# A recurrent attention loop on one core: the last K copied and transposed in two halves, one mask copy moved forward

## The chip, the cores and the metric

The kernel runs on one core of one Trainium2 chip. The metric is the device time of one execution in microseconds; runs of the same kernel are compared by their median. In the profile, PE is TensorE's matmuls, PEld its weight loads, DVE is VectorE, ACT is ScalarE, POOL is GpSimd and SP the engine that issues most DMAs. All times are microseconds unless marked ns; L495 is line 495 of the kernel.

## The reference, cut to what matters

Two blocks on `x` of 2048 tokens by 512. The first, which holds the change, is attention over segments of 32 tokens with a memory of 8 tokens that each segment hands to the next. With the shapes put in (32 heads of 128, 64 segments):

```python
mask = (idx[:, None] < M) | (idx[:, None] >= idx[None, :])   # L = 8 + 32 = 40 positions
mem = mem0
for s in range(n_seg):                                       # 64 segments, one after the other
    h = concatenate([mem, x[:, s*32:(s+1)*32]], axis=1)
    q, k, v = (einsum('btd,dhe->bhte', h, W) for W in (Wq, Wk, Wv))
    p = softmax(where(mask, einsum('bhqe,bhke->bhqk', q, k) * scale, -1e9))
    o = einsum('bhte,hed->btd', einsum('bhqk,bhke->bhqe', p, v), Wo)
    mem = o[:, :8]
    outs.append(o[:, 8:])
h = x + concatenate(outs)           # x goes into the loop layer-normed
```

The second block is a gated MLP with a 2048 by 2048 mixing over tokens: `h + ((z1 * (w_sp @ layernorm(z2) + b_sp)) @ w_out)` with `z1, z2` the halves of `gelu(layernorm(h) @ w_in)`. Everything is bf16 in memory.

## The kernel before, in words

The kernel is one straight list of operations. A small recorder (`Emitter`) takes each with the engine that it runs on and the tokens that it reads and writes, and puts a semaphore wait where a token's last writer or reader was on another engine. Within an engine the order is the order of the code, so what stands ahead of an operation on its queue is set by hand. A token of a PSUM bank, `("ps", bank)`, also makes a reader on one engine wait for earlier readers on another.

After a start phase the loop over the 64 segments begins (L926). Each of them depends on the one before by the 8 memory rows (`hT`, columns 0 to 7). Heads are worked on in two halves b = 0 and 1 of 16 heads each. One segment does, in this order of code:

1. **Q and K** (`QK`, L501): for each half, Q and K of the 8 memory rows and the segment's first 24 tokens (the last 8 tokens' projections are made for 16 segments at a time by the filling work), 16 matmuls of 512 columns each. Four matmuls go to four column groups of TensorE at a time. The bank is `QKB[(b, mi)]`: 0 for Q of half 0, 1 for K of half 0, 6 and 7 for half 1.
2. **Copy and transposition** (`QK_evac`, L512): ScalarE copies the bank from PSUM into `Tst` in bf16, in an order of columns that puts two heads into one 32-bit word (L515). VectorE then transposes the words, 32 by 32 at a time, into `QT` (L521) or `KT` (L524). `Tst` has one buffer for Q and one for K. This happens four times in a segment: Q0, K0, Q1, K1; K1 is the "last K".
3. **Mask** (`mask_put`, L534): VectorE writes the mask into the bank in which the scores of that half are then summed: bank 0 for half 0 and bank 1 for half 1, free again once Q0 and K0 have been copied. Half 0's mask copy stands after the transposition of Q0. Half 1's stands after that of Q1.
4. **Scores of half 0** (`S_half`, L538; matmuls L546 and L552), **exp of half 0** (L560, ScalarE), V matmuls (`V_half`), the softmax **sums of half 0** (L567 and the held ones at L496, TensorE, with a matrix of ones), **ln of half 0** (L578).
5. **Scores of half 1**, **exp of half 1**, then the reciprocal of half 0's sums as an exp (L582), the rest of V's half 1, **sums of half 1**, ln and reciprocal of half 1.
6. Normalising of the probabilities: half 0 on POOL, half 1 on VectorE (L586, L590). Ahead of half 0's POOL also copies the next segment's part of `QT` (L531), after the scores have read the old one.
7. A filling piece of other work for TensorE (projections for later segments, or parts of the second block), then **P·V** of both halves (L615, L621), their copies (`cT`), the output projection `Wo`, and the memory rows for the next segment.

In the first segment whole groups of V matmuls stand between the last K and the scores of half 0. After the loop comes the second block's mixing, which the change does not touch.

ScalarE's queue around the change is: copies of Q0, K0, Q1, K1, exp 0, ln 0, exp 1, reciprocal 0, ln 1, reciprocal 1. VectorE's queue is: transposition of Q0, mask 0, transposition of K0, transposition of Q1, mask 1, transposition of K1, copy of V 0, copy of V 1, normalising of half 1.

Of the kernel before, what the change touches and what calls it, by code (L numbers as in the profile page):

```python
# [8 lines left out]
U32 = mybir.dt.uint32  # L9
ACT = mybir.ActivationFunctionType  # L10
# [159 lines left out]
def fast_path(nc, st, keep, A_x, A_mem0, A_Wq, A_Wk, A_Wv, A_Wo, A_seg_len, B_w_in, B_w_sp, B_b_sp, B_w_out, out):  # L170
# [26 lines left out]
    def sb(name, shape, dt):  # L197
        return st.enter_context(nc.sbuf_tensor("f_" + name, shape, dt))
# [18 lines left out]
    QT = sb("QT", [128, 2, 8, 40, 2], BF)  # L217
    KT = sb("KT", [128, 2, 8, 32, 2], BF)
    Tst = sb("Tst", [128, 2, 512], BF)
# [40 lines left out]
    ps = st.enter_context(nc.psum_tensor("f_ps", [128, 8, 512], F32))  # L260
# [5 lines left out]
    def PB(b):  # L266
        return ("ps", b)
# [4 lines left out]
    def pe(fn, **k):  # L272
        return em.add("pe", fn, **k)

    def act(fn, **k):
        return em.add("act", fn, **k)

    def dve(fn, **k):
        return em.add("dve", fn, **k)
# [221 lines left out]
    def QK(s, b, mi, dcs, first, last, held=None):  # L501
        ws = (w_q, w_k)[mi]
        bank = QKB[(b, mi)]
        sl = slot(s)
        for dc in dcs:
            for c in range(4):
                rhs = ws[:, dc, :].rearrange("p (h c i) -> p c h i", c=4, i=32)[:, c, 16 * b:16 * b + 16, :]
                pe(lambda e, dc=dc, c=c, rhs=rhs: tile_mm(e, ps[32 * c:32 * c + 32, bank, :], hT[:, sl, dc, :], rhs,
                                                          dc == first, dc == last, c, dc == held),
                   reads=[("hTx", (s // 4) % 3), ("hTm", s, dc // 2), ("W", mi, 2 * b), ("W", mi, 2 * b + 1)], writes=[PB(bank)])  # L510

    def QK_evac(s, b, mi):  # L512
        bank = QKB[(b, mi)]
        tb = mi
        act(lambda e: e.activation(out=Tst[:, tb, :].rearrange("p (hp i r) -> p hp i r", i=32, r=2),  # L515
                                   in_=ps[:, bank, :].rearrange("p (hp r i) -> p hp i r", r=2, i=32), func=ACT.Copy),
            reads=[PB(bank)], writes=[("T", tb)])
        src = Tst[:, tb, :].bitcast(U32)
        if mi == 0:
            dst = QT[:, b, :, :, :].rearrange("p hp q r -> p (hp q r)").bitcast(U32).rearrange("p (hp q) -> p hp q", hp=8)[:, :, 8:40]  # L520
            dve(lambda e: e.transpose(out=dst, in_=src), reads=[("T", tb)], writes=[("QT", b)])  # L521
        else:
            dst = KT[:, b, :, :, :].rearrange("p hp q r -> p (hp q r)").bitcast(U32)
            dve(lambda e: e.transpose(out=dst, in_=src), reads=[("T", tb)], writes=[("KT", b)])  # L524

    def qx_copy(s):
        j = s % CK
# [6 lines left out]
    def mask_put(b):  # L534
        bank = SBK[b]
        dve(lambda e: e.tensor_copy(out=ps[:, bank, 0:224], in_=mask[:, :]), reads=["mask"], writes=[PB(bank)])  # L536

    def S_half(s, b):  # L538
        bank = SBK[b]
        j = s % CK  # L540
        buf = (s // CK) % 2
        rd = [("QT", b), ("KT", b), ("QTe", b)]
        for g in range(4):
            for c in range(4):
                hp, r = 2 * c + g // 2, g % 2
                pe(lambda e, hp=hp, r=r, c=c, g=g: e.matmul(  # L546
                    ps[32 * c:32 * c + 32, bank, g * 40:(g + 1) * 40], lhsT=KT[:, b, hp, :, r], rhs=QT[:, b, hp, :, r],
                    start=False, stop=(g == 3), skip_group_check=True, tile_position=(0, 32 * c)),
                    reads=rd, writes=[PB(bank)])
        for c in range(4):  # L550
            h0 = 16 * b + 4 * c
            pe(lambda e, c=c, h0=h0: e.matmul(  # L552
                ps[32 * c:32 * c + 32, bank, 160:224], lhsT=QTx[buf][:, 1, j, h0:h0 + 4, :].rearrange("p h k -> p (h k)"),
                rhs=QT[:, b, 2 * c:2 * c + 2, 0:16, :].rearrange("p hp q r -> p hp r q"),
                start=False, stop=True, skip_group_check=True, tile_position=(0, 32 * c)),
                reads=rd + [("QTx", buf, 1, i) for i in range(8)], writes=[PB(bank)])
# [369 lines left out]
    for s in range(NSEG):  # L926
# [16 lines left out]
        QK(s, 0, 1, (1, 0), 1, 2, None if s else 1)  # L943
        QK(s, 0, 0, (2, 3), 0, 3)
        QK_evac(s, 0, 0)
        mask_put(0)
        QK(s, 0, 1, (3, 2), 1, 2, 3)
        QK_evac(s, 0, 1)
        for mi in range(2):
            QK(s, 1, mi, ((2, 0, 1, 3), (3, 0, 1, 2))[mi], (2, 3)[mi], (3, 2)[mi], (2, 3)[mi])  # L950
            lastop["qk"[mi]] = em.by_eng["pe"][-1]
            QK_evac(s, 1, mi)
            if mi == 0:
                mask_put(1)
        if s == 0:
            ebank[:] = [3, 4, 5]
            for n in range(2):
                start_v(n)
        S_half(s, 0)
        sm_exp(0)  # L960
        V_half(s, 0, (0,))
# [4 lines left out]
        sm_sums(0)  # L966
        sm_ln(0)
        S_half(s, 1)
        lastop["s"] = em.by_eng["pe"][-1]
        sm_exp(1)  # L970
# [291 lines left out]
    for tb in range(NTB):  # L1262
        for fb in range(len(ACC) if tb == 0 else 0, FB):
            if tb == 0:
                bank = 5 + fb % 3
            else:
                bank = gcnt % 2
# [693 lines left out]
def build_kernel(nc, A_x, A_mem0, A_Wq, A_Wk, A_Wv, A_Wo, A_seg_len, B_x, B_w_in, B_w_sp, B_b_sp, B_w_out, out):  # L1961
    args = (A_x, A_mem0, A_Wq, A_Wk, A_Wv, A_Wo, A_seg_len, B_w_in, B_w_sp, B_b_sp, B_w_out, out)
    with contextlib.ExitStack() as keep:
        with contextlib.ExitStack() as st:
            em, sems, dsems, flag = fast_path(nc, st, keep, *args)
# [88 lines left out]
```

## Time and profile before

| | us |
|---|---|
| runs, median of 3 | 860.34 |
| runs, lowest and highest | 859.93, 861.05 |
| the profiled execution's own time | 860.99 |
| its span, first to last instruction | 859.2 |
| granted TensorE clock | 1.00 of full speed |

The loop runs from about 36 us (first copy of a Q) to about 696 us. A steady segment takes 10.1 us, of which the stretch that the change touches, from the first copy of a Q to the second sums, is about 4 us. The timeline's columns are the start in us from the beginning of the span, the duration in us, engine, line, operation, tiles out<-in, shape, and the number of instructions that one row merges; a bracket at the end is idle time of the engine just before and what ended it. A row of merged matmuls has as its duration the time from the first start to the last modelled end; since ends overlap the next starts, starts are the better measure on PE. Rows of groups have the sum of busy time, then the mean in ns of one instruction, then the idle time before them.

### The profile page before, as it was taken

The numbers are of one execution on the slowest core, as the hardware profiler recorded it, in microseconds if no ns is written. First come the engines' busy times: TensorE is split into PE (matmuls) and PEld (weight loads), VectorE is DVE, ScalarE is ACT, GpSimd is POOL, SyncE is SP. The second block draws the span as 40 slices with busy tenths as digits, with TensorE's granted clock in tenths as the row PEclk, the third lists the DMA queues.
The fourth block names the chain that finished last, engine by engine and source line by source line (L and its number), as shares of the span: only waits on it lengthen the run. The fifth ranks groups of instructions, "written<-read, shape, count | busy, mean of one in ns | idle before, by whom it ended". The sixth has DMA issues, their size and how long they took to land.

```text
span 859.2 us, 43589 instructions
## 1 busy us (share of the span) xinstructions
PE 841.9 (98%) x20849; PEld 443.5 (52%) x19061; DVE 532.6 (62%) x1191; ACT 422.1 (49%) x1085; POOL 158.3 (18%) x404
## 2 busy tenths in 40 slices
PE   6999999999999999999999999999999999999998
PEld 5754445555555555555555555454554444444443
DVE  3455677666766666676766666666666658363443
ACT  2455565555555555555555555455655576400000
POOL 5111121122211212121212121112211114100000
PEclk9999999999999999999999999999999999999999
DMA  9972312213202113132212121533222299032101
GB/s 316 379 222 59 73 56 56 60 40 87 59 25 74 44 56 61 32 65 47 61 37 62 38 59 46 111 74 77 75 63 68 63 229 350 20 106 90 50 13 39
DMA packets 105181, 76.08 MB, mean 89 GB/s; under 512 B 64024, under 2 KB 90528, under 8 KB 104992
## 3 DMA queue, kind: packets, MB, share of 16 engines
q1 hardware_dynamic: 104992, 73.24, 30.2%
q8 instruction: 158, 2.59, 1.3%
q14 instruction: 31, 0.25, 0.1%
HBM read 41.69 MB, written 20.91 MB: 73 GB/s over the span
## 4 chain that ended last, share of the span: by engine, by line
PE 95%; DVE 2%; DMA 1%; issue 1%; POOL 1%; ACT 0%; SPq 0%; POOLq 0%
PE f_ps L495 46%; PE f_ps L1152 11%; PE f_ps L496 8%; PE f_ps L414 7%; PE f_ps L699 4%; PE f_ps L1246 3%; PE f_ps L615 3%; PE f_ps L433 2%; PE f_ps L1145 2%; PE f_ps L546 2%; PE f_ps L758 2%; PE f_ps L567 1%; DVE f_st L1127 1%; PE f_ps L621 1%; PE f_ps L439 1%; PE f_ps L672 1%
## 5 line engine op out<-in xcount | busy, mean ns | idle before, releaser
L495 PE MATMUL f_ps<-f_arena,f_hT 128*32 128x512 bf16 x5120 | 359.3, 380 | 0.3
L495 PEld LDWEIGHTS f_ps<-f_arena,f_hT 128*32 128x32 bf16 x5120 | 114.9, 95 | 155.5 <-issue 63.1
L515 ACT ACTIVATE f_Tst<-f_ps 128x512 bf16<-128x512 f32 x256 | 145.9, 596 | 77.5 <-PE f_ps L495 77.3
L495 PE MATMUL f_ps<-f_arena,f_cT 128*32 128x256 bf16 x3844 | 127.9, 273 | 1.9 <-issue 1.3
L495 PEld LDWEIGHTS f_ps<-f_arena,f_cT 128*32 128x32 bf16 x3844 | 94.1, 96 | 32.6 <-ACT f_cT L634 22.7
L521 DVE STREAM_TRANSPOSE f_QT<-f_Tst 128x256 uint32<-128x256 uint32 x128 | 57.0, 446 | 84.1 <-ACT f_Tst L515 84.1
L607 DVE CAST f_V_sb<-f_ps 128x512 bf16<-128x512 f32 x128 | 88.5, 692 | 24.6 <-PE f_ps L495 16.3
L1152 PE MATMUL f_ps<-f_arena 128*128 128x512 bf16 x448 | 99.6, 379 | 0.0
L496 PE MATMUL f_ps<-f_arena,f_hT 128*32 128x512 bf16 x1024 | 99.5, 379 | 0.0
L531 POOL COPY f_QT<-f_arena 128x256 bf16<-128x256 bf16 x64 | 30.6, 478 | 315.1 <-PE f_ps L552 315.1
L634 ACT ACTIVATE f_cT<-f_ps 128x320 bf16<-128x320 f32 x128 | 49.0, 435 | 51.2 <-PE f_ps L621 51.2
L636 DVE TENSOR_SCALAR f_cT<-f_ps 128x320 bf16<-128x320 f32 x128 | 56.9, 486 | 25.4 <-PE f_ps L621 25.4
L1152 PEld LDWEIGHTS f_ps<-f_arena 128*128 128x128 bf16 x448 | 43.6, 98 | 52.7
L414 PE MATMUL f_ps<-f_hTe,f_arena 128*128 128x128 bf16 x1024 | 67.1, 223 | 2.7 <-DMA f_arena<-in_A_Wq_dram 1.8
L665 DVE CAST f_part<-f_ps 128x256 bf16<-128x256 f32 x64 | 27.2, 425 | 68.6 <-PE f_ps L495 68.6
L414 PEld LDWEIGHTS f_ps<-f_hTe,f_arena 128*128 128x128 bf16 x1024 | 59.2, 99 | 8.0 <-issue 2.2
L524 DVE STREAM_TRANSPOSE f_KT<-f_Tst 128x256 uint32<-128x256 uint32 x128 | 55.3, 432 | 7.9
L578 ACT ACTIVATE f_R_sb<-f_ps 128x160 f32<-128x160 f32 x128 | 38.8, 303 | 39.8 <-PE f_ps L496 32.2
L1158 DVE TENSOR_TENSOR f_arena<-f_ps,f_arena 128x512 f32<-128x512 f32 x28 | 19.3, 690 | 60.7 <-PE f_ps L1152 60.7
L677 ACT ACTIVATE f_hT<-f_ps 128x16 bf16<-128x16 f32 x126 | 23.1, 183 | 55.0 <-PE f_ps L672 54.6
L663 ACT ACTIVATE f_part<-f_ps 128x256 bf16<-128x256 f32 x64 | 24.5, 383 | 48.2 <-PE f_ps L495 48.2
L536 DVE CAST f_ps<-f_mask 128x224 f32<-128x224 bf16 x128 | 47.0, 367 | 0.0
(120 smaller groups left out, 1084.3 us busy)
## 6 DMA issues: line engine op xcount, KB each, us to landing
wT_d<-f_wst SPq DMA_DIRECT2D x32, 256.0 KB, 2.4
f_arena<-wT_d SPq DMA_DIRECT2D x32, 256.0 KB, 4.8
f_arena<-in_A_Wq_dram SPq DMA_DIRECT2D x4, 1024.0 KB, 9.0
f_arena<-in_A_Wk_dram SPq DMA_DIRECT2D x4, 1024.0 KB, 14.4
f_arena<-in_A_Wv_dram SPq DMA_DIRECT2D x4, 1024.0 KB, 14.5
f_arena<-in_A_Wo_dram SPq DMA_DIRECT2D x8, 512.0 KB, 9.5
f_Vx<-vext_d SPq DMA_DIRECT2D x63, 64.0 KB, 2.9
vext_d<-f_Vs SPq DMA_DIRECT2D x24, 128.0 KB, 2.0
```

What stands on the lines that cost most here:

```text
L414: pe(lambda e, h=h, dc=dc, hh=hh: e.matmul(ps[:, bank, hh * 128:(hh + 1) * 128], lhsT=ws[:, dc, h * DH:(h + 1) * DH], rhs=hTe[:, ck % 3, d ...
L495: return e.matmul(out, lhsT=lhsT, rhs=rhs, start=start, stop=stop, skip_group_check=True, tile_position=(0, 32 * c))
L496: return e.add_instruction(mybir.InstMatmult(name=nc.get_next_instruction_name(), ins=[e.lower_ap(rhs), e.lower_ap(lhsT)], outs=[e.lower_a ...
L515: act(lambda e: e.activation(out=Tst[:, tb, :].rearrange("p (hp i r) -> p hp i r", i=32, r=2), in_=ps[:, bank, :].rearrange("p (hp r i) -> ...
L521: dve(lambda e: e.transpose(out=dst, in_=src), reads=[("T", tb)], writes=[("QT", b)])
L524: dve(lambda e: e.transpose(out=dst, in_=src), reads=[("T", tb)], writes=[("KT", b)])
L536: dve(lambda e: e.tensor_copy(out=ps[:, bank, 0:224], in_=mask[:, :]), reads=["mask"], writes=[PB(bank)])
L578: act(lambda e: e.activation(out=R_sb[:, b, :], in_=ps[:, bank, 224:384], func=ACT.Ln, scale=LNS), reads=[PB(bank)], writes=[("R", b)])
L607: dve(lambda e: e.tensor_copy(out=V_sb[:, b, :], in_=ps[:, bank, :]), reads=[PB(bank)], writes=[("V", b)])
L634: act(lambda e: e.activation(out=dst, in_=src, func=ACT.Copy, scale=UNSC), reads=[PB(PVB[c])], writes=[("cT", c)])
L636: dve(lambda e: e.tensor_scalar(out=dst, in0=src, scalar1=UNSC, scalar2=None, op0=ALU.mult), reads=[PB(PVB[c])], writes=[("cT", c)])
L1152: pe(lambda e: e.matmul(ps[:, bank, 0:TB], lhsT=z2[:, sc, fb * 128:(fb + 1) * 128], rhs=wTb[tb % 2][:, :, sc, :], start=(n == 0), stop=(n ...
```

## The change

Three things differ. `QK_evac` takes a number of parts. With two parts it copies the bank in two instructions of 256 columns and transposes in two instructions of 128 words (half of a row each), and each transposition waits only for its own half of the copy. The loop calls it with two parts for the last K of a segment (`1 + mi` with `mi` = 1) and with one for the other three. `mask_put(1)` is called ahead of Q and K of half 1, so that it stands on VectorE between the transposition of K0 and that of Q1. The tokens of `T` and `KT` are split in two accordingly; the scores of a half read both parts of `KT`. After it ScalarE's queue has K1a, K1b ahead of exp 0, and VectorE's: Q0, mask 0, K0, mask 1, Q1, K1a, K1b.

```diff
-    def QK_evac(s, b, mi):
+    def QK_evac(s, b, mi, parts=1):
         bank = QKB[(b, mi)]
         tb = mi
-        act(lambda e: e.activation(out=Tst[:, tb, :].rearrange("p (hp i r) -> p hp i r", i=32, r=2),
-                                   in_=ps[:, bank, :].rearrange("p (hp r i) -> p hp i r", r=2, i=32), func=ACT.Copy),
-            reads=[PB(bank)], writes=[("T", tb)])
-        src = Tst[:, tb, :].bitcast(U32)
...
+        n = 8 // parts
+        for k in range(parts):
+            tok = [("T", tb, 0), ("T", tb, 1)] if parts == 1 else [("T", tb, k)]
+            cs = slice(64 * n * k, 64 * n * (k + 1))
+            act(lambda e, cs=cs: e.activation(out=Tst[:, tb, cs].rearrange("p (hp i r) -> p hp i r", i=32, r=2),
+                                              in_=ps[:, bank, cs].rearrange("p (hp r i) -> p hp i r", r=2, i=32), func=ACT.Copy),
+                reads=[PB(bank)], writes=tok)
+        for k in range(parts):
+            tok = [("T", tb, 0), ("T", tb, 1)] if parts == 1 else [("T", tb, k)]
+            src = Tst[:, tb, 64 * n * k:64 * n * (k + 1)].bitcast(U32)
+            hs = slice(n * k, n * (k + 1))
...
+            else:
+                dst = KT[:, b, hs, :, :].rearrange("p hp q r -> p (hp q r)").bitcast(U32)
+                wr = [("KT", b, 0), ("KT", b, 1)] if parts == 1 else [("KT", b, k)]
+            dve(lambda e, dst=dst, src=src: e.transpose(out=dst, in_=src), reads=tok, writes=wr)
...
-        rd = [("QT", b), ("KT", b), ("QTe", b)]
+        rd = [("QT", b), ("KT", b, 0), ("KT", b, 1), ("QTe", b)]
...
         QK_evac(s, 0, 1)
+        mask_put(1)
         for mi in range(2):
             QK(s, 1, mi, ((2, 0, 1, 3), (3, 0, 1, 2))[mi], (2, 3)[mi], (3, 2)[mi], (2, 3)[mi])
             lastop["qk"[mi]] = em.by_eng["pe"][-1]
-            QK_evac(s, 1, mi)
-            if mi == 0:
-                mask_put(1)
+            QK_evac(s, 1, mi, 1 + mi)
```

More of the change, by code (lines that the diff above doesn't have):

```diff
@@ L510, in QK @@
                    reads=[("hTx", (s // 4) % 3), ("hTm", s, dc // 2), ("W", mi, 2 * b), ("W", mi, 2 * b + 1)], writes=[PB(bank)])
-    def QK_evac(s, b, mi):
+    def QK_evac(s, b, mi, parts=1):
         bank = QKB[(b, mi)]
         tb = mi
-        act(lambda e: e.activation(out=Tst[:, tb, :].rearrange("p (hp i r) -> p hp i r", i=32, r=2),
-                                   in_=ps[:, bank, :].rearrange("p (hp r i) -> p hp i r", r=2, i=32), func=ACT.Copy),
-            reads=[PB(bank)], writes=[("T", tb)])
-        src = Tst[:, tb, :].bitcast(U32)
-        if mi == 0:
[L520 to L524, printed above, removed]
+        n = 8 // parts
[9 more added lines that the diff above has]
+            hs = slice(n * k, n * (k + 1))
+            if mi == 0:
+                dst = QT[:, b, hs, :, :].rearrange("p hp q r -> p (hp q r)").bitcast(U32).rearrange("p (hp q) -> p hp q", hp=n)[:, :, 8:40]
+                wr = [("QT", b)]
+            else:
+                dst = KT[:, b, hs, :, :].rearrange("p hp q r -> p (hp q r)").bitcast(U32)
+                wr = [("KT", b, 0), ("KT", b, 1)] if parts == 1 else [("KT", b, k)]
+            dve(lambda e, dst=dst, src=src: e.transpose(out=dst, in_=src), reads=tok, writes=wr)
     def qx_copy(s):
@@ L951, in fast_path @@
             lastop["qk"[mi]] = em.by_eng["pe"][-1]
-            QK_evac(s, 1, mi)
-            if mi == 0:
-                mask_put(1)
+            QK_evac(s, 1, mi, 1 + mi)
         if s == 0:
```

## The prediction

> **What bounds the kernel now.** I read the page first, then the table of waits, then the timeline of single engines in one steady segment. The page names the engine:
>
> ```profile
> span 859.2 us, 43589 instructions
> ...
> PE 841.9 (98%) x20849; PEld 443.5 (52%) x19061; DVE 532.6 (62%) x1191; ACT 422.1 (49%) x1085; POOL 158.3 (18%) x404
> ...
> PE 95%; DVE 2%; DMA 1%; issue 1%; POOL 1%; ACT 0%; SPq 0%; POOLq 0%
> ```
>
> TensorE is busy for 98% of the span and carries 95% of the last-ending chain, so only an edit that shortens a pause of TensorE can pay. But matmul ends are modelled and overlap the next start, so short pauses do not appear as idle time. The waits of the weight loads name one partner around the change, the sums' wait for exp:
>
> ```profile
> PEld f_ps L567 <- ACT f_E_sb L560: 35.5, 126, 0.4
> ```
>
> No row says that the scores (L546) wait. Pauses have to be read from the distance of matmul starts. This is segment 53 on TensorE, from the first softmax sums (L567) to the second P·V:
>
> ```profile
> 589.70 0.24 PE L567 MATMUL f_ps<-f_E_sb,f_ones 128*32 128x160 bf16 x4
> 589.77 0.20 PE L496 MATMUL f_ps<-f_E_sb,f_ones 128*32 128x64 bf16 x4
> 589.84 0.28 PE L546 MATMUL f_ps<-f_QT,f_KT 128*32 128x40 bf16 x16
> ...
> 590.64 0.25 PE L567 MATMUL f_ps<-f_E_sb,f_ones 128*32 128x160 bf16 x4
> ...
> 591.80 0.27 PE L615 MATMUL f_ps<-f_E_sb,f_V_sb 32*128 32x40 bf16 x16
> ...
> 592.07 0.27 PE L615 MATMUL f_ps<-f_E_sb,f_V_sb 32*128 32x40 bf16 x16
> ```
>
> The same stretch on VectorE, with the K and Q transpositions (L524, L521) and mask copies (L536), and on ScalarE: the copy of the last K (L515), exp of half 0 (L560), ln of half 0 (L578), exp of half 1 (L560).
>
> ```profile
> 587.55 0.37 DVE L536 CAST f_ps<-f_mask 128x224 f32<-128x224 bf16 x1
> 587.83 0.42 DVE L524 STREAM_TRANSPOSE f_KT<-f_Tst 128x256 uint32<-128x256 uint32 x1
> 588.48 0.45 DVE L521 STREAM_TRANSPOSE f_QT<-f_Tst 128x256 uint32<-128x256 uint32 x1 [0.23 <-ACT f_Tst L515]
> 588.85 0.36 DVE L536 CAST f_ps<-f_mask 128x224 f32<-128x224 bf16 x1
> 589.34 0.45 DVE L524 STREAM_TRANSPOSE f_KT<-f_Tst 128x256 uint32<-128x256 uint32 x1
> ```
>
> ```profile
> 588.71 0.60 ACT L515 ACTIVATE f_Tst<-f_ps 128x512 bf16<-128x512 f32 x1 [0.27 <-PE f_ps L495]
> 589.21 0.35 ACT L560 ACTIVATE f_E_sb<-f_ps 128x224 bf16<-128x224 f32 x1
> 590.01 0.30 ACT L578 ACTIVATE f_R_sb<-f_ps 128x160 f32<-128x160 f32 x1 [0.45 <-PE f_ps L496]
> 590.23 0.36 ACT L560 ACTIVATE f_E_sb<-f_ps 128x224 bf16<-128x224 f32 x1
> ```
>
> Read together: the last K is copied until 589.31, transposed from 589.34 to 589.79, and the scores of half 1 start at 589.84, 0.05 behind the transposition. The second sums start at 590.64, 0.05 behind the end of exp 1 (590.23 + 0.36 = 590.59). Both times the operand came last. How large is the first pause? Segment 52 is one of the few in which the scores follow the sums sooner:
>
> ```profile
> 579.64 0.24 PE L567 MATMUL f_ps<-f_E_sb,f_ones 128*32 128x160 bf16 x4
> ...
> 579.75 0.28 PE L546 MATMUL f_ps<-f_QT,f_KT 128*32 128x40 bf16 x16
> ...
> 580.56 0.25 PE L567 MATMUL f_ps<-f_E_sb,f_ones 128*32 128x160 bf16 x4
> ...
> 581.72 0.27 PE L615 MATMUL f_ps<-f_E_sb,f_V_sb 32*128 32x40 bf16 x16
> ...
> 581.99 0.27 PE L615 MATMUL f_ps<-f_E_sb,f_V_sb 32*128 32x40 bf16 x16
> ```
>
> ```profile
> 579.96 0.30 ACT L578 ACTIVATE f_R_sb<-f_ps 128x160 f32<-128x160 f32 x1 [0.49 <-PE f_ps L496]
> 580.15 0.35 ACT L560 ACTIVATE f_E_sb<-f_ps 128x224 bf16<-128x224 f32 x1
> ```
>
> Sums to scores is 0.11 there against 0.14 in segment 53, so the pause at the scores is at least 0.03. But from the first sums to the second it is 0.92 against 0.94: of the pause that is gone, a part comes back ahead of the second sums. Segment 52 is therefore the model of what the change makes of every segment.
>
> **The change, part by part.** Three edits: the last K's copy becomes two of 256 columns, its transposition two of 128 words, and the second mask copy goes ahead of the second Q's transposition. Their rows:
>
> ```profile
> L607 DVE CAST f_V_sb<-f_ps 128x512 bf16<-128x512 f32 x128 | 88.5, 692 | 24.6 <-PE f_ps L495 16.3
> ...
> L665 DVE CAST f_part<-f_ps 128x256 bf16<-128x256 f32 x64 | 27.2, 425 | 68.6 <-PE f_ps L495 68.6
> ...
> L663 ACT ACTIVATE f_part<-f_ps 128x256 bf16<-128x256 f32 x64 | 24.5, 383 | 48.2 <-PE f_ps L495 48.2
> ```
>
> The copy: ScalarE takes 0.383 for 256 columns from PSUM (L663) and 0.60 for 512. Instructions behind one another overlap: exp 0 starts 0.50 after the copy's start, that is 0.10 before its end. So a half holds ScalarE for 0.28, and the two for 0.56 instead of 0.50. The halves start at 588.71 and 588.99 and end at 589.09 and 589.37. Queued behind them is exp 0, which moves from 589.21 to 589.27 and ends at 589.62; the first sums can then start at 589.67. TensorE comes to them at 589.70, when its V matmuls are through. So the extra 0.06 is hidden, with 0.03 to spare; without that cover it would cost 0.06 per segment.
>
> The transposition: no row shows 128 words. Its bounds are half of a full one, 0.22, and a full one, 0.45. VectorE's casts fall from 692 to 425 ns from 512 to 256 columns, about 1.04 ns per column on top of a fixed part; with that slope 128 words fewer are 0.13 less, 0.31. I take that, being the same engine's own rate. The halves start at 589.12 and, behind the second copy, at 589.37 + 0.03 = 589.40; the first lies under the second copy. The second ends at 589.71, so the scores could start at 589.76, where TensorE is free for them only at 589.70 + 0.11 = 589.81. At 0.22 they could at 589.67, still useless; at 0.38 they start at 589.83 or so, as now; at 0.45 at 589.90, 0.06 later than now. So up to 0.36 the pause is gone.
>
> The mask copy: it held VectorE from 588.85, where nothing waited for it in time. A cast is followed 0.28 after its start (587.55 to 587.83). The first K's transposition starts at 587.83 and, overlapping as the others do (0.37 from one start to the next, 588.48 to 588.85), lets the mask start at about 588.20 at the latest; 588.20 + 0.28 = 588.48 is where the second Q's transposition starts today, released by ScalarE. So the move costs nothing, or a few hundredths ahead of a Q that is needed only with the last K. The mask needs the bank of the first K, whose copy is over before that K's transposition starts. No DMA is moved, and the SP and POOL queues keep their order; POOL's copy for the next segment follows the scores, which come earlier.
>
> What is late next: exp 1 stands behind ln 0 on ScalarE, and ln 0 follows the first sums, which do not move. In segment 53 exp 1 starts 0.22 after ln 0, in segment 52 0.19, where it lasts 0.35 and not 0.36. So exp 1 can end 0.03 to 0.04 earlier and no more; TensorE finishes its V matmuls earlier than that and waits. By the starts of the sums the gain is 0.94 − 0.92 = 0.02. I take 0.028 between these readings. Behind the second sums nothing is lost: to the P·V of half 0 it is 1.16 in both segments and to that of half 1 1.43.
>
> The sum: the first of the 64 segments puts whole V groups between K and scores and gains nothing; 63 × 0.028 = 1.76 us. Against the profiled execution, 860.99 with a span of 859.2, this is 859.2 with a span of 857.4. The median of the runs, 860.34, is 0.65 below the profiled execution, within the runs' own spread; the same subtraction from it gives **858.6 us**. With 0.02 to 0.035 per segment it is 1.3 to 2.2 us, so this case's own range is 858.1 to 859.1.
>
> **The rivals.** First, *the whole pause counts*. If the 0.22 between ln 0 and exp 1 was set by the scores alone, all that the scores gain reaches the second sums: 0.03 to 0.05 each, at most 63 × 0.05 = 3.1 us, 857.2. For it: exp 1 does move when the scores do. Against it: in segment 52 the scores came 0.03 earlier and the sums 0.02, and exp 1 then starts 0.11 before the end of ln 0, while the copy and exp 0 overlap by 0.10: there is hardly more room between two instructions of ScalarE.
>
> Second, *the wait only changes its place*. If half a transposition costs 0.38, or if the wait ahead of the second sums takes back all of the gain, the time stays 860.3. Segment 52 speaks against the latter; nothing but VectorE's rate on other shapes speaks against the former. At the far bound of 0.45 the scores come 0.06 later, 63 × 0.06 = 3.8 us, 864.1.
>
> Third, slower: *the halves of the copy do not overlap*, on ScalarE, and delay exp 0 and with it the first sums. Then they hold ScalarE for 2 × 0.383 = 0.77; exp 0 starts at 589.48 instead of 589.21, ends at 589.83, and the sums start at 589.88 instead of 589.70. That is 0.18 lost and 0.028 still gained, 63 × 0.152 = 9.6 us, 869.9. It begins to cost when a half holds ScalarE for over 0.295 and outweighs the gain over about 0.31; the forecast has 0.28. Against it: the copy and exp 0 overlap by 0.10, though there the two read different banks, while the halves read one.
>
> [...]
>
> **How the numbers follow.** A measurement of this kernel can tell about 0.2%, 1.72 us, from no change. The forecast has a chance of 0.73; its 1.76 lies hardly above that line, so I give 0.48 to more and 0.25 to less. The whole pause: 0.08, faster. The wait changes its place: 0.10, of it 0.07 the same and 0.03 slower. The copies do not overlap: 0.09, slower. Faster 0.56, same 0.32, slower 0.12. The range runs from 857.2 (the whole pause) to 860.4 (no change, with the spread of the runs); it leaves out the slower cases, 0.12.
>
> **What would show it.** In the timeline after: scores of half 1 about 0.10 to 0.11 behind the first sums; the two copies about 0.28 apart with 0.38 each; half a transposition of 0.31; exp 1 0.19 to 0.20 behind ln 0; the second sums 0.91 to 0.92 behind the first in nearly all segments. The total wait of the second sums' weight loads on exp should rise. I am wrong if the first sums move away from the V matmuls ahead of them, if half a transposition takes over 0.36, or if the segment's later part stretches by what its middle gained.

## The result and the profile after

In interleaved runs the changed kernel has a median of 858.38 us (12 runs, 857.05 to 859.93) against 860.15 for the kernel before (12 runs, 858.79 to 861.62). The ratio is 0.9972, with a 95% interval of 0.9963 to 0.9982: 1.5 to 3.2 us faster. The forecast was 858.6. The profiled execution has a time of 858.17 and a span of 855.9, against 860.99 and 859.2 before.

First the page after and, of its groups with the shapes kept apart, those of the change: the whole copies and transpositions that remain (128x512, 128x256) and the halves (128x256, 128x128). Then the wait of the sums' weight loads for exp.

```profile
span 855.9 us, 43707 instructions
...
PE 839.7 (98%) x20839; PEld 444.6 (52%) x19061; DVE 537.9 (63%) x1255; ACT 424.3 (50%) x1149; POOL 158.4 (19%) x404
```

```profile
L519 ACT ACTIVATE f_Tst<-f_ps 128x512 bf16<-128x512 f32 x192 | 107.7, 595 | 60.7 <-PE f_ps L495 60.7
...
L519 ACT ACTIVATE f_Tst<-f_ps 128x256 bf16<-128x256 f32 x128 | 42.1, 381 | 16.9 <-PE f_ps L495 16.8
...
L532 DVE STREAM_TRANSPOSE f_KT<-f_Tst 128x128 uint32<-128x128 uint32 x128 | 37.6, 312 | 12.9 <-ACT f_Tst L519 12.9
```

```profile
PEld f_ps L575 <- ACT f_E_sb L568: 41.6, 126, 0.4
```

Last the weight loads of the scores, before (L546) and after (L554); the last number is the idle time before them:

```profile
L546 PEld LDWEIGHTS f_ps<-f_QT,f_KT 128*32 128x32 bf16 x2048 | 27.7, 95 | 22.6 <-issue 0.6
```

```profile
L554 PEld LDWEIGHTS f_ps<-f_QT,f_KT 128*32 128x32 bf16 x2048 | 28.5, 95 | 14.6 <-issue 0.6
```

ScalarE and VectorE each have 64 instructions more and are busy for longer (2.2 and 5.3 us), while the span is shorter: neither sets the end. A half is copied in 0.381 and transposed in 0.312. The weight loads of the sums (L575, before L567) wait 41.6 us for exp, where it was 35.5. Summed by halves from the two traces, about 4 us of the 6.1 stand at half 0, whose sums start no later for it, and 2 at half 1, where the forecast looked for the rise.

The weight loads of the scores show the pause after all: of their 22.6 us of idle time 8.2 stood at half 1, 128 ns in a usual segment; after the change 0.2 stand there. The table of waits names only 0.6 of the 22.6, so the place can be seen only in the row's total. The row does not give the size: with the copy split alone (below) half 1 has 8.2 again, though the scores come 62 ns later than before.

Segment 53 again, on TensorE from the V matmuls ahead of the first sums to the second sums, then ScalarE and VectorE. Lines have moved: L554 are the scores, L568 exp, L586 ln, L544 the mask, L532 both transpositions. A row with x2 is two merged instructions.

```profile
586.36 0.82 PE L495 MATMUL f_ps<-f_arena,f_hT 128*32 128x512 bf16 x12
587.00 0.24 PE L575 MATMUL f_ps<-f_E_sb,f_ones 128*32 128x160 bf16 x4
587.07 0.20 PE L496 MATMUL f_ps<-f_E_sb,f_ones 128*32 128x64 bf16 x4
587.10 0.27 PE L554 MATMUL f_ps<-f_QT,f_KT 128*32 128x40 bf16 x16
...
587.24 0.82 PE L495 MATMUL f_ps<-f_arena,f_hT 128*32 128x512 bf16 x12
587.92 0.25 PE L575 MATMUL f_ps<-f_E_sb,f_ones 128*32 128x160 bf16 x4
```

```profile
586.02 0.66 ACT L519 ACTIVATE f_Tst<-f_ps 128x256 bf16<-128x256 f32 x2 [0.27 <-PE f_ps L495]
586.56 0.36 ACT L568 ACTIVATE f_E_sb<-f_ps 128x224 bf16<-128x224 f32 x1
587.32 0.30 ACT L586 ACTIVATE f_R_sb<-f_ps 128x160 f32<-128x160 f32 x1 [0.39 <-PE f_ps L496]
587.51 0.35 ACT L568 ACTIVATE f_E_sb<-f_ps 128x224 bf16<-128x224 f32 x1
```

```profile
585.13 0.42 DVE L532 STREAM_TRANSPOSE f_KT<-f_Tst 128x256 uint32<-128x256 uint32 x1
585.48 0.37 DVE L544 CAST f_ps<-f_mask 128x224 f32<-128x224 bf16 x1
585.78 0.45 DVE L532 STREAM_TRANSPOSE f_QT<-f_Tst 128x256 uint32<-128x256 uint32 x1
586.43 0.59 DVE L532 STREAM_TRANSPOSE f_KT<-f_Tst 128x128 uint32<-128x128 uint32 x2 [0.20 <-ACT f_Tst L519]
```

The last half of K is transposed at 587.02 (586.43 + 0.59), 0.08 before the scores at 587.10; in the kernel before, the scores started 0.05 behind it, as soon as they could. They now start 0.10 behind the first sums and not 0.14: TensorE comes straight from the sums. The same stretch before had these V matmuls:

```profile
589.05 0.82 PE L495 MATMUL f_ps<-f_arena,f_hT 128*32 128x512 bf16 x12
...
589.99 0.82 PE L495 MATMUL f_ps<-f_arena,f_hT 128*32 128x512 bf16 x12
```

Ahead of the first sums, where nothing holds them, the sums start 0.64 behind the start of 12 V matmuls (586.36 to 587.00; 647 ns in the median). Ahead of the second sums it was 655 ns before and is 686 now (587.24 to 587.92): the second sums start 0.05 to 0.06 behind the end of exp 1 (587.51 + 0.35), and TensorE waits 0.04 for it, where it waited 0.01. From first to second sums it is 0.92 instead of 0.94.

Rows have steps of 0.01. The traces' own starts, as medians over the 63 segments behind the first, give the same with one digit more. They are the measure in all that follows (ns; the first column is from the first scores of a segment to the first sums, P·V is that of half 1, the last is the ratio to the kernel before on the same chip, with its interval):

| kernel | scores 0 to sums 0 | sums 0 to scores 1 | sums 0 to sums 1 | sums 1 to second P·V | ratio |
|---|---|---|---|---|---|
| before | 1210 | 143 | 943 | 1428 | 1 |
| after | 1210 | 97 | 917 | 1427 | 0.9972 (0.9963 to 0.9982) |
| after, again | 1210 | 97 | 917 | 1426 | 0.9984 (0.9974 to 0.9994) |
| halves alone | 1210 | 97 | 917 | 1426 | 0.9979 (0.9970 to 0.9989) |
| mask alone | 1210 | 144 | 944 | 1429 | 1.0000 (0.9987 to 1.0013) |
| copy split alone | 1211 | 205 | 1003 | 1431 | 1.0033 (1.0021 to 1.0046) |
| transposition split alone | 1210 | 203 | 1003 | 1427 | 1.0030 (1.0011 to 1.0048) |
| quarters | 1313 | 108 | 927 | 1428 | 1.0061 (1.0037 to 1.0085) |
| ln 0 behind exp 1 | 1210 | 98 | 888 | 1687 | 1.0100 (1.0083 to 1.0117) |

The gain is 26 ns per segment, over 63 segments 1.6 us, or a ratio of 0.9981. That lies in the intervals of all three comparisons of a kernel with the halves, and none of the three reaches 1.

### The profile page after: what moved, and what is told of

It is laid out like the page before. It is cut to its first block, busy times and chain, and to the rows that moved or that the text cites. A ratio compares the mean times of both kernels' runs of the same rounds, so it can differ in the third digit from the quotient of the medians.

```text
span 855.9 us, 43707 instructions
## 1 busy us (share of the span) xinstructions
PE 839.7 (98%) x20839; PEld 444.6 (52%) x19061; DVE 537.9 (63%) x1255; ACT 424.3 (50%) x1149; POOL 158.4 (19%) x404
## 4 chain that ended last, share of the span: by engine, by line
PE 95%; DVE 2%; DMA 1%; issue 1%; POOL 1%; ACT 0%; SPq 0%; POOLq 0%
PE f_ps L495 46%; PE f_ps L1159 11%; PE f_ps L496 8%; PE f_ps L414 7%; PE f_ps L707 4%; PE f_ps L1253 3%; PE f_ps L623 3%; PE f_ps L433 2%; PE f_ps L1152 2%; PE f_ps L766 2%; PE f_ps L554 1%; PE f_ps L575 1%; DVE f_st L1134 1%; PE f_ps L629 1%; PE f_ps L439 1%; PE f_ps L680 1%
## 5 line engine op out<-in xcount | busy, mean ns | idle before, releaser
L519 ACT ACTIVATE f_Tst<-f_ps 128x512 bf16<-128x512 f32 (+1 forms) x320 | 149.8, 509 | 77.6 <-PE f_ps L495 77.4
L532 DVE STREAM_TRANSPOSE f_QT<-f_Tst 128x256 uint32<-128x256 uint32 x128 | 57.0, 446 | 67.8 <-ACT f_Tst L519 67.7
L532 DVE STREAM_TRANSPOSE f_KT<-f_Tst 128x128 uint32<-128x128 uint32 (+1 forms) x192 | 64.5, 348 | 12.9 <-ACT f_Tst L519 12.9
L586 ACT ACTIVATE f_R_sb<-f_ps 128x160 f32<-128x160 f32 x128 | 38.8, 303 | 36.0 <-PE f_ps L496 35.9
L544 DVE CAST f_ps<-f_mask 128x224 f32<-128x224 bf16 x128 | 47.0, 368 | 0.0
```

Source lines behind the costliest of these rows:

```text
L519: act(lambda e, cs=cs: e.activation(out=Tst[:, tb, cs].rearrange("p (hp i r) -> p hp i r", i=32, r=2), in_=ps[:, bank, cs].rearrange("p (h ...
L532: dve(lambda e, dst=dst, src=src: e.transpose(out=dst, in_=src), reads=tok, writes=wr)
L586: act(lambda e: e.activation(out=R_sb[:, b, :], in_=ps[:, bank, 224:384], func=ACT.Ln, scale=LNS), reads=[PB(bank)], writes=[("R", b)])
```

## The experiments

**The halves alone.** The mask copy goes back to its place behind the second Q's transposition.

```diff
-        mask_put(1)
         for mi in range(2):
...
             QK_evac(s, 1, mi, 1 + mi)
+            if mi == 0:
+                mask_put(1)
```

> The halves alone; the second mask copy stands where it was, behind the second Q's transposition. My theory (the last K's copy and transposition are what the scores of half 1 wait for, the mask copy is hidden in either place): scores of half 1 start 0.10 behind the first sums (before 0.14, after 0.10), second sums 0.917 behind the first (before 0.943, after 0.917), time equal to the full change, 1.6 us under before. Rival (the mask copy delays the first half's transposition and with it the second): second sums 0.93 to 0.94 behind the first and under half of the gain.

The segment is that of the full change to the nanosecond of the medians: 97 and 917. VectorE's timeline shows why:

```profile
585.83 0.45 DVE L532 STREAM_TRANSPOSE f_QT<-f_Tst 128x256 uint32<-128x256 uint32 x1 [0.23 <-ACT f_Tst L519]
586.20 0.37 DVE L544 CAST f_ps<-f_mask 128x224 f32<-128x224 bf16 x1
586.48 0.59 DVE L532 STREAM_TRANSPOSE f_KT<-f_Tst 128x128 uint32<-128x128 uint32 x2
```

The mask fits between the Q and the first half of K, which then follows without idle time but not late: the two halves take 0.59 from start to end, as in the full change.

**The mask alone.** On the kernel before: the mask copy ahead, the last K whole.

```diff
         QK_evac(s, 0, 1)
+        mask_put(1)
         for mi in range(2):
...
             QK_evac(s, 1, mi)
-            if mi == 0:
-                mask_put(1)
```

> The move of the second mask copy alone; the last K is copied and transposed whole. My theory: nothing changes, scores 0.14 behind the first sums, second sums 0.943 behind the first, 860.2 us, within 0.1% of before. Rival (the mask copy counts): a part of the 1.6 us is there already, second sums under 0.93.

```profile
589.63 0.24 PE L567 MATMUL f_ps<-f_E_sb,f_ones 128*32 128x160 bf16 x4
...
589.78 0.28 PE L546 MATMUL f_ps<-f_QT,f_KT 128*32 128x40 bf16 x16
...
590.58 0.25 PE L567 MATMUL f_ps<-f_E_sb,f_ones 128*32 128x160 bf16 x4
```

144 and 944, ratio 1.0000: nothing. The two edits are settled: the halves are all of the gain, and the mask copy is free in either place.

**The change once more**, without an edit.

> The changed kernel once more, to size the gain. My theory: 63 segments by 0.026 us, 1.6 us, ratio 0.998. Rival (something beside the middle of the segments gains, as the first profile's 3.3 us of span suggest): ratio 0.997 or less again, and the stretch from the second P.V of a segment to the next segment's first scores shorter in the median than 6.56 us.

The segments are the same, the ratio is 0.9984, and the median from the second P·V to the next segment's first scores is 6.56 as before. The rival is not borne out.

**The copy split alone**: two copies, then one whole transposition. The line stands ahead of the loop over the transpositions.

```diff
+        parts, n = 1, 8
         for k in range(parts):
```

> The changed kernel with the copy in two halves, but one whole transposition behind both. My theory: the copy ends 0.05 later, so K is ready 0.05 later than before; scores 0.19 behind the first sums (before 0.14), second sums 0.99 behind the first (before 0.943), 63 x 0.05 = 3.3 us slower than before, 863.4. The first sums stay 1.21 behind the first scores of the segment. Rival (splitting the copy is what pays): not slower than before.

```profile
591.40 0.66 ACT L519 ACTIVATE f_Tst<-f_ps 128x256 bf16<-128x256 f32 x2 [0.27 <-PE f_ps L495]
591.94 0.36 ACT L569 ACTIVATE f_E_sb<-f_ps 128x224 bf16<-128x224 f32 x1
```

```profile
592.38 0.24 PE L576 MATMUL f_ps<-f_E_sb,f_ones 128*32 128x160 bf16 x4
...
592.59 0.28 PE L555 MATMUL f_ps<-f_QT,f_KT 128*32 128x40 bf16 x16
...
593.39 0.25 PE L576 MATMUL f_ps<-f_E_sb,f_ones 128*32 128x160 bf16 x4
```

The copies end at 592.06, 0.66 behind their start, where one whole copy takes 0.60. Scores and second sums come 0.06 later than in the kernel before, where 0.05 had been expected, and 63 × 0.06 = 3.8 us is within the interval's 1.8 to 4.0. The first sums do not move: the longer hold of ScalarE is hidden from them. Nothing starts on the first half here, so two halves only cost.

**The transposition split alone**: one copy, then two transpositions. The first two lines stand ahead of the loop over the copies, the last behind it.

```diff
-        n = 8 // parts
+        want, parts, n = parts, 1, 8
...
+        parts, n = want, 8 // want
```

> The changed kernel with the copy whole and the transposition in two halves behind it. My theory: the second half starts 0.23 behind the first and takes 0.3, so K is ready 0.08 to 0.10 later than before; scores 0.22 to 0.25 behind the first sums, second sums 1.02 to 1.05 behind the first, 5 to 6.5 us slower than before, 865 to 867. Rival (two short transpositions cost no more than one): scores as in before, 860.

```profile
590.88 0.51 DVE L533 STREAM_TRANSPOSE f_KT<-f_Tst 128x128 uint32<-128x128 uint32 x2 [0.42 <-ACT f_Tst L519]
```

The direction is as expected, the size is not: 203 and 1003, 60 ns per segment and not 80 to 100. The two take 0.51 together. The second, queued behind the first, takes 269 ns (median), where a half that has to wait for its operand takes 311. The measured 2.6 us (0.9 to 4.1) agrees with 63 × 0.06 = 3.8.

**Quarters**: four copies of 128 columns and four transpositions of 64 words. The tokens of `T` and `KT` are split in four as well (not shown).

```diff
-            QK_evac(s, 1, mi, 1 + mi)
+            QK_evac(s, 1, mi, 1 + 3 * mi)
```

> The changed kernel with the last K in four parts instead of two. My theory: a copy of 128 columns takes 0.27 and holds ScalarE for 0.165, four of them 0.66 instead of 0.54, so exp of half 0 ends too late for the first sums, which come 0.07 to 0.08 later (1.28 to 1.29 behind the first scores of the segment instead of 1.21); the scores of half 1 stay 0.10 behind the first sums and the second sums 0.917; 63 x (0.08 - 0.026) = 3.4 us slower than before, 863.5. Rival (finer pieces only bring K earlier): no slower than after.

```profile
593.00 0.79 ACT L519 ACTIVATE f_Tst<-f_ps 128x128 bf16<-128x128 f32 x4 [0.27 <-PE f_ps L495]
593.64 0.39 ACT L568 ACTIVATE f_E_sb<-f_ps 128x224 bf16<-128x224 f32 x1
```

```profile
593.34 0.82 PE L495 MATMUL f_ps<-f_arena,f_hT 128*32 128x512 bf16 x12
594.09 0.25 PE L575 MATMUL f_ps<-f_E_sb,f_ones 128*32 128x160 bf16 x4
```

Here the condition of the forecast's third rival holds, by more copies instead of less overlap: the first sums come late. Exp 0 starts 0.64 behind the first copy and lasts 0.39 instead of 0.35; it ends at 594.03, and the sums follow at 594.09. By the 0.64 of the changed kernel the V matmuls ahead of them were through at 593.98 (593.34 + 0.64), so TensorE stands for 0.11. K itself is early enough: the scores follow the sums closely (108 ns, 11 more than with two halves; no run here shows why). Sum: 103 − 16 = 87 ns per segment, 5.5 us; measured 5.3 (3.2 to 7.3). The expectation said 0.07 to 0.08 for the late sums, because exp 0's own longer time was not in it. A copy of 128 columns takes 0.282 in the mean, where 0.27 was expected, and the four hold ScalarE for 0.64, where 0.66 was expected.

**ln 0 behind exp 1**, on the changed kernel.

```diff
         sm_sums(0)
-        sm_ln(0)
...
         sm_exp(1)
+        sm_ln(0)
         sm_rcp(0)
```

> The changed kernel with ln of half 0 put behind exp of half 1 on ScalarE. My theory (exp of half 1 is now held by ln of half 0, so that of the 0.046 gained at the scores 0.02 are lost ahead of the second sums): second sums 0.89 behind the first instead of 0.917, so the middle gains another 0.03. But the reciprocal of half 0 and then ln of half 1 come later, by my sum 0.07 per segment at the second P.V, so the whole is slower than after: 861 to 864 us. Rival (exp of half 1 is held by the scores alone): second sums stay at 0.917.

```profile
595.89 0.36 ACT L568 ACTIVATE f_E_sb<-f_ps 128x224 bf16<-128x224 f32 x1 [0.56 <-PE f_ps L560]
596.14 0.30 ACT L586 ACTIVATE f_R_sb<-f_ps 128x160 f32<-128x160 f32 x1
```

```profile
595.41 0.24 PE L575 MATMUL f_ps<-f_E_sb,f_ones 128*32 128x160 bf16 x4
...
596.30 0.25 PE L575 MATMUL f_ps<-f_E_sb,f_ones 128*32 128x160 bf16 x4
...
597.50 0.27 PE L623 MATMUL f_ps<-f_E_sb,f_V_sb 32*128 32x40 bf16 x16
597.95 0.21 PE L629 MATMUL f_ps<-f_E_sb,f_Vx 32*128 32x64 bf16 x4 [0.17 <-POOL f_E_sb L598]
```

```profile
PEld f_ps L629 <- POOL f_E_sb L598: 16.1, 63, 0.3
```

The theory's first half holds to the number. Exp 1 now waits for the scores (its bracket names L560) and the second sums come 0.89 behind the first, 888 in the median: the 29 ns that ln 0 held back are there. That exp 1 stood behind ln 0 is thereby shown, and with it where the rest of the 46 had gone. The second half was right in sign and too small: the second P·V comes 260 ns later and not 70. I had only followed VectorE's normalising of half 1. The bracket of L629 names the other chain: the late reciprocal delays POOL's normalising of half 0, and its second part (L598) now arrives last, 63 times of 63. Against the kernel before that is 204 ns per segment up to the second P·V (55 gained, 259 lost), 12.9 us; about 4 of it come back in the stretch from there to the next segment's scores, whose mean is 6.53 instead of 6.59. The whole is 8.6 us slower (7.2 to 10.1), where 861 to 864 us had been expected. So no version better than the changed kernel comes out of this; ln 0 stays where it is.

## Why the prediction was right

*The place.* The scores of half 1 waited for the last K, 46 ns per segment; the kernel with the mask alone and the one with the halves alone leave no other cause. The prediction says that no row shows the scores waiting; that holds for the table of waits and for the matmuls, but the idle time of the scores' weight loads shows it. The size of the pause could be read only from starts. Segment 52 gave it as at least 0.03; it was 0.046.

*The copy.* Forecast 0.383 and a hold of 0.28; measured 0.381, and exp 0 starts 543 ns behind the first half, 272 per half. Exp 0 started 0.05 later, lasted 365 ns instead of 352 and so ended 0.06 later, hidden as forecast: the first sums start 1210 ns behind the scores in both kernels. Of the cover this left 24 ns (77 ns from the end of exp 0 to the first sums, against 53 where sums follow exp at once).

*The transposition.* Forecast 0.31, by the slope of VectorE's casts from PSUM, 1.04 ns per column; measured 0.312. That this slope would hold for a transposition from SBUF was an assumption, and it did: 134 ns from 256 words to 128, 66 from 128 to 64.

*The mask.* Forecast free, and it was: 144 and 944 with the mask alone, against 143 and 943.

*What is late next.* This was the step that gave the size. That the second sums gain only about 0.028, because ln 0 is ahead of exp 1, was taken from one odd segment of the trace before, and the number was a choice between readings of 0.02 and 0.03 to 0.04. The mechanism held: 222 ns from the start of ln 0 to that of exp 1 became 200 in all 64 segments, and with ln 0 out of the way the second sums come another 29 ns earlier. That the choice came within 2 ns of the 26 is in part luck, as the rows have steps of 10 ns. One thing was not in the sum: where the scores do not wait for K, the V matmuls follow them sooner, 133 ns behind the first score instead of 144. So the V matmuls start 57 ns earlier, and the longer wait for exp 1 (39 ns instead of 9) takes back 30. The first rival (the whole pause counts) is thereby out: 26 of 46 ns arrive.

*The overlap of the two halves.* The third rival did not come about. Measured, a second half starts 0.28 behind the first, although the first lasts 0.38, also on one bank. So 0.10 of each copy is covered, and a second copy costs ScalarE 0.05 (543 ns against 493 up to exp 0). Four quarters hold it for 0.64, where one whole copy holds it for 0.49.

*The size.* 63 × 0.028 = 1.76 us was forecast; 63 × 0.026 = 1.6 is what the segments show. The medians differ by 1.77, the ratio of the first comparison gives 2.4 and that of the second 1.4; that the first medians fit the forecast to 0.01 is luck, and so in part is 858.38 against 858.6, since the changed kernel's median was 860.07 in the second comparison, where the kernel before had 861.47. The first profile's span is 3.3 us shorter, more than the segments explain: 0.4 lies ahead of the second segment, 0.3 behind the last P·V, and about 0.8 in the stretches from the second P·V to the next scores, whose mean is 6.58 against 6.59 us at equal medians (6.56). That mean is 6.61 with the mask alone, where nothing changed. It is moved by few segments: between the first two profiles 55 of the 62 stretches agree within 0.03, and seven differ by 0.17 to 1.20, one of them the other way. What moves those from one execution to another stays open.

## What to carry to other kernels

On an engine that is busy for 98%, look at the idle time of the weight loads for the place and at distances between starts for the size, and compare a usual round of the loop with an odd one that had its operand early: the odd one shows what the change would give, and what would take part of it back. Splitting a copy and what follows it paid here only when both were split, and only as long as the engine's next instruction had room for the extra hold: two pieces fitted, four did not. A pause that goes is worth what the next wait leaves of it, here 26 of 46 ns.

## What was not expected of the hardware

Exp of half 0 lasts longer in the profile behind more and shorter copies: 352 ns behind one copy, 365 behind two halves and 388 behind four quarters. On VectorE a transposition that stood ready in the queue was shorter than one that had to wait for its operand (420 against 445 ns for 256 words, 269 against 311 for 128). The place in the queue alone does not make it: in the kernel with the halves alone the first half follows the mask copy without idle time, its operand having come only just then, and lasts 311 as well. Why, no run here shows. The first belonged in the sums of the quarters, the second in those of the split transposition, and neither was there.
